# Weights times values, two heads at a time in fp32, each head in its own 64 columns of the array

## The chip, the cores and the metric

The program runs on one core of a Trainium2 chip. The metric is the device time of one launch, in microseconds, from the runs of the whole program. Beside it there is one profiled execution, whose span (first to last instruction) and whose instruction times the readings below use. The engines are called as in the profile: PE (TensorE, matmuls), PEld (its weight loads), DVE (VectorE), ACT (ScalarE), POOL (GpSimd), SP (the engine that issues the DMAs).

## The reference

Attention with a compressive memory over 4 batches of 8 heads, 576 tokens, head width 64, followed by a dense block with 2,048 hidden units. All in float32.

```python
def _attn_ref(q, k, v, M_prev, z_prev, beta):
    scores = scale * np.matmul(q, k.transpose(0, 1, 3, 2))
    scores = np.where(causal, -1000000000.0, scores)
    scores = scores - scores.max(-1, keepdims=True)
    a = np.exp(scores)
    a /= a.sum(-1, keepdims=True) + 1e-09
    local = np.matmul(a, v)
    q_p = phi(q)
    mem_ret = np.einsum('bhsd,bhde->bhse', q_p, M_prev)
    mem_norm = np.einsum('bhsd,bhd->bhs', q_p, z_prev)[..., None] + 1e-06
    g = 1.0 / (1.0 + np.exp(-beta))[None, :, None, None]
    return g * (mem_ret / mem_norm) + (1 - g) * local

def _moe_ref(x, w_in, w_out):            # x: 2304 x 512
    h = x @ w_in
    sp = np.where(h > 20.0, h, np.log1p(np.exp(np.minimum(h, 20.0))))
    return (h * np.tanh(sp)) @ w_out
```

## The kernel before

There are 32 heads in 16 pairs (`p`), two heads (`e` = 0, 1) to a pair. Per head, `scores` multiplies q by k, DVE adds the mask and takes the row minimum (L458), ACT takes the exponential (L465), `norm` scales each row by its weight (L101) and puts the features of q beside it, so that one row of `w` holds both the attention weights and the part that multiplies the memory. `transp` transposes `w` on PE in four groups of three or four blocks (L534), and a copy brings each group from PSUM to SBUF. `av` then multiplies: the values (with the memory matrix as their first 64 rows) are the stationary operand, 128 rows by 64 columns, and the transposed weights move. The output of a head is 64 x 576, made in two parts: part 0 holds 320 tokens (three matmuls of 320, 256 and 128 columns), part 1 holds 256 tokens (five matmuls, four of 256 columns and one of 128); the table is `AVJ`. Both parts use the one PSUM bank of the pool `ps_v`, so part 1 begins after ACT has copied part 0 out (L105, into the tile `x` of the pair, 64 partitions to a head).

`av` has two forms here, and `FA` = 16 tells them apart:

- Heads 0 to 15: plain fp32. Transposed weights `at` are copied out alternately by ACT and DVE (`FAE`), and each of the eight matmuls of a head (L570) takes them and `v` as they are. In the trace one such fp32 matmul stands as two instructions.
- Heads 16 to 31: split operands. ACT rounds the transposed weights to `ah`, DVE makes the rest `al` (L543), POOL makes `vh` from `v` in the same way (`vprep`, L109 and L95), and each of the eight products is three matmuls of one instruction each (L583): 24 for a head.

Both forms write PSUM partitions 0 to 63, so both use columns 0 to 63 of the array.

Beside the heads, six blocks of `w_in` and `w_out` are converted to pairs of rounded operands (`split`, `narrow`, L141 to L173: DVE ops L148, L154, L157, L164 among them), one after each of the heads 1 to 6. From head 9 on, one step of the dense block's first part (`steps_a`) is issued per head: 18 slots `slot_a` of 24 matmuls (L257), each followed by a chain of element-wise work on ACT, DVE and POOL (`mish0` to `mish2`), and 12 calls of `out_a`, 18 matmuls each (L272). These steps run at a low priority (`p1`: -400). When the heads are done, `tail` converts the ten remaining weight blocks, mixed with what is left of the first part, and runs 62 units: 12 matmuls `mm_h` (L697), the same element-wise chain, and 9 or 12 matmuls `mm_o` (L717).

The order of the instructions on each engine is made by a scheduler when the program is built, from the order of the code, the priorities (`OFF`, through `run`) and its own estimate of when things are ready. It is fixed in the program: each engine works through its own list and waits where an operand isn't there.

## Time and profile before

| | us |
|---|---|
| median of 3 runs | 764.65 (764.34 to 766.92) |
| span of the profiled execution | 763.0 |
| the profiled execution's PE busy | 708.4 |
| DVE busy | 647.2 |
| POOL busy | 436.0 |
| ACT busy | 409.2 |

The profiled execution's span lies 1.65 us below the median of the runs. In the page, busy time of an engine is the time that it had an instruction in work; a share of the span near 100% in a stretch says that the stretch waits for that engine, if others wait for it. Matmuls are pipelined, so the step from one's start to the next one's start tells what it costs, and not its duration. In a timeline row, "x10" merges ten instructions in sequence, and the next row's start tells when they were over.

### The profile page before, as it was taken

The numbers are of one execution on the slowest core, as the hardware profiler recorded it, in microseconds if no ns is written. First come the engines' busy times: TensorE is split into PE (matmuls) and PEld (weight loads), VectorE is DVE, ScalarE is ACT, GpSimd is POOL, SyncE is SP. The second block draws the span as 40 slices with busy tenths as digits, with TensorE's granted clock in tenths as the row PEclk, the third lists the DMA queues.
The fourth block names the chain that finished last, engine by engine and source line by source line (L and its number), as shares of the span: only waits on it lengthen the run. The fifth ranks groups of instructions, "written<-read, shape, count | busy, mean of one in ns | idle before, by whom it ended". The sixth has DMA issues, their size and how long they took to land.

```text
span 763.0 us, 11170 instructions
## 1 busy us (share of the span) xinstructions
PE 708.4 (93%) x3544; PEld 557.0 (73%) x3544; DVE 647.2 (85%) x1287; ACT 409.2 (54%) x929; POOL 436.0 (57%) x442
## 2 busy tenths in 40 slices
PE   5999999999999999999778677699999999999996
PEld 3566666667788888878666555478888889899894
DVE  5799998999987787868999999978868877786885
ACT  5566765767576766657453533344434445445443
POOL 4787886888889687756757665643223313223221
PEclk9999999999999999999999897899999999999999
DMA  6566786655644564333636222033033030021001
GB/s 244 163 187 198 225 235 182 204 159 161 199 119 145 149 166 140 93 104 128 207 128 209 78 89 83 29 110 111 0 111 111 12 113 16 1 82 43 1 1 41
DMA packets 51851, 91.18 MB, mean 119 GB/s; under 512 B 8272, under 2 KB 23632, under 8 KB 51792
## 3 DMA queue, kind: packets, MB, share of 16 engines
q1 hardware_dynamic: 51792, 90.47, 38.9%
q8 instruction: 28, 0.46, 0.2%
q14 instruction: 31, 0.25, 0.1%
HBM read 56.63 MB, written 17.30 MB: 97 GB/s over the span
## 4 chain that ended last, share of the span: by engine, by line
PE 62%; DVE 23%; issue 6%; ACT 3%; DMA 3%; POOL 1%; SPq 0%; POOLq 0%; ACTq 0%; DVEq 0%
PE o L717 10%; PE h L697 10%; PE vps L570 7%; PE t L534 7%; PE s L450 7%; PE h L257 5%; PE s L449 5%; PE vps L583 4%; PE acc L272 4%; DVE u L92 4%; DVE ws L148 3%; DVE r L92 2%; DVE g L95 2%; DVE wa L154 2%; DVE ws L164 2%
## 5 line engine op out<-in xcount | busy, mean ns | idle before, releaser
L95 POOL TENSOR_TENSOR u<-u,r 128x512 f32<-128x512 f32 (+1 forms) x80 | 106.5, 1331 | 205.4 <-DVE r L92 191.8
L697 PE MATMUL h<-xb,wi 128*128 128x384 f32 (+1 forms) x744 | 173.1, 379 | 22.9 <-DVE u L233 22.8
L697 PEld LDWEIGHTS h<-xb,wi 128*128 128x128 f32 x744 | 141.4, 196 | 46.3 <-DVE u L233 24.6
L717 PE MATMUL o<-wo,g 128*128 128x512 f32 x648 | 163.1, 394 | 4.1 <-ACT g L105 3.1
L717 PEld LDWEIGHTS o<-wo,g 128*128 128x128 f32 x648 | 122.3, 190 | 29.7 <-ACT g L105 3.9
L228 ACT ACTIVATE L<-u 128x512 f32<-128x512 f32 (+1 forms) x80 | 47.1, 589 | 149.5 <-DVE u L92 148.0
L465 ACT ACTIVATE w<-w,mx 128x576 f32<-128x576 f32 (+4 forms) x160 | 88.9, 557 | 33.3 <-DVE mx L458 33.0
L101 POOL TENSOR_SCALAR w<-w,rc 128x64 f32<-128x64 f32 (+3 forms) x128 | 84.2, 674 | 14.2 <-DVE rc L504 10.0
L458 DVE CUSTOM_DVE_ANT_0 w<-s,mask 128x288 f32<-128x288 f32 (+4 forms) x160 | 62.6, 422 | 28.0 <-PE s L450 16.9
L92 DVE SCALAR_TENSOR_TENSOR u<-e 128x512 f32<-128x512 f32 (+1 forms) x80 | 81.0, 1013 | 1.3
L534 PE MATMUL t<-ident,w 128*128 128x128 f32 (+1 forms) x417 | 72.3, 288 | 7.3 <-DVE al L543 6.2
L233 DVE SCALAR_TENSOR_TENSOR u<-u,h 128x512 f32<-128x512 f32 (+1 forms) x80 | 50.1, 626 | 30.0 <-POOL u L95 29.9
L92 DVE SCALAR_TENSOR_TENSOR L<-u,r 128x512 f32<-128x512 f32 (+1 forms) x80 | 57.4, 717 | 18.6 <-ACT r L229 18.2
L257 PE MATMUL h<-xb,wi 128*128 128x256 f32 x432 | 65.9, 291 | 2.5 <-DVE u L233 2.5
L272 PE MATMUL acc<-wo,g 128*128 128x512 f32 x216 | 62.0, 418 | 3.8 <-ACT ob L105 3.2
L450 PE MATMUL s<-lk,r 64*128 64x288 f32 (+1 forms) x168 | 64.7, 385 | 0.0
L534 PEld LDWEIGHTS t<-ident,w 128*128 128x128 f32 (+1 forms) x417 | 48.3, 144 | 22.4 <-DVE al L543 6.8
L449 PE MATMUL s<-r 128*128 128x288 f32 (+1 forms) x168 | 60.2, 358 | 1.1 <-DVE mx L458 1.1
L257 PEld LDWEIGHTS h<-xb,wi 128*128 128x128 f32 x432 | 56.4, 190 | 6.2 <-DVE u L233 3.1
L570 PE MATMUL vps<-at,v 128*64 128x256 f32 (+2 forms) x256 | 59.9, 373 | 0.0
L105 ACT CAST g<-u 128x512 fp32r<-128x512 f32 (+1 forms) x80 | 45.8, 573 | 20.7 <-DVE u L233 19.4
L92 DVE SCALAR_TENSOR_TENSOR r<-L,r 128x512 f32<-128x512 f32 (+1 forms) x80 | 55.1, 689 | 0.3
(72 smaller groups left out, 1280.0 us busy)
## 6 DMA issues: line engine op xcount, KB each, us to landing
r<-t SPq DMA_DIRECT2D x84, 144.0 KB, 2.7
raw<-in_w_in_dram SPq DMA_DIRECT2D x16, 512.0 KB, 3.5
raw<-in_w_out_dram SPq DMA_DIRECT2D x16, 512.0 KB, 3.7
f<-in_f_src_dram SPq DMA_DIRECT2D x14, 576.0 KB, 5.2
xb<-xs SPq DMA_DIRECT2D x24, 256.0 KB, 4.6
qn<-in_qn_dram SPq DMA_DIRECT2D x16, 320.0 KB, 3.2
v<-in_vn_dram SPq DMA_DIRECT2D x16, 320.0 KB, 4.0
xs<-xo SPq DMA_DIRECT2D x16, 288.0 KB, 2.9
```

The costliest lines, as they stand in the source:

```text
L92: engines[ENG[name]].scalar_tensor_tensor(**kw)
L95: engines[ENG[name]].tensor_tensor(**kw)
L101: engines[which].tensor_scalar(out=o, in0=i, scalar1=scale, scalar2=1.0, op0=ALU.mult, op1=ALU.mult)
L257: nc.tensor.matmul(ps[:, TA * a:TA * a + TA], wi[y, f][:, c, :], x[c][:, z], start=(q == 0), stop=(q == 11))
L272: nc.tensor.matmul(acc[:], g[:, y, c:c + 128], wo[z, f], start=(f == 0 and y == z), stop=(f == KA - 1 and z == 1),)
L449: nc.tensor.matmul(ps[:, o:o + n], r[:, e, q0:q0 + 128], r[:, 2 + e, a:b], start=True, stop=False)
L450: nc.tensor.matmul(ps[:, o:o + n], r[le, e, q0:q0 + 128], l[le, a:b], start=False, stop=True)
L465: nc.scalar.activation(out=row, in_=row, func=ACTF.Exp, scale=-1.0, bias=g["mx"][:, m:m + 1], accum_out=g["sm"][:, m:m + 1])
L534: nc.tensor.transpose(ps[:, o:o + n], g["w"][:n, c:c + 128], ident[:n, :n])
L570: nc.tensor.matmul(ps[0:64, a:b], d["v"][:, t, e], g["ah"][gi][:, c:c + b - a], start=(k == 0), stop=(k == last))
L697: nc.tensor.matmul(ps[:, :n], wi[a, f][:, c, :], x[c][:, b], start=(k == 0), stop=(k == 11))
L717: nc.tensor.matmul(D_[t][:], g[:, y, 128 * t:128 * t + 128], wo[z, f], start=(f == f0 and y == z), stop=(f == NF - 1 and z == 1),)
```

## The change

All pairs now use plain fp32, and a pair's two heads are multiplied together. `av` takes a pair: it runs once, after the second head's `transp`, and for each of the eight products issues a matmul for head 0 into PSUM partitions 0 to 63 (array columns 0 to 63) and one for head 1 into partitions 64 to 127 (columns 64 to 127), in turn. ACT copies a part of both heads with one instruction over 128 partitions. The split operands go: no `vh` (and no `vprep` on POOL), no `al` on DVE. Heads 16 to 31 get their transposed weights like the others, two groups by ACT and two by DVE. The `at` tiles get 14 buffers in one tag (before: five each in two), `v` gets two. The core of the diff:

```diff
-AHB = 5
+AHB = 14
...
-VB = 1
+VB = 2
...
-F2 = 32
...
-FA = 16
...
         def loadv(p):
             d = pr[p]
-            if 2 * p < FA:
-                d["v"] = ap_.tile([128, 5, 2, 2, D], F32, tag="vh", name="v")[:].rearrange(
-                    "p t e i d -> p (t e i d)")[:, 0:640].rearrange("p (t e d) -> p t e d", t=5, e=2)
-            else:
-                d["v"] = ap_.tile([128, 5, 2, D], F32, tag="v", name="v", bufs=VB)[:]
+            d["v"] = ap_.tile([128, 5, 2, D], F32, tag="v", name="v", bufs=VB)[:]
...
-        def vprep(p):
...
-            return [lambda: one(0), lambda: two(0), lambda: one(1), lambda: two(1)] if 2 * p >= FA else []
...
-            def hi(base, n):
-                copy(FAE[base] if h < FA else "a", g["ah"][base][:, :n], g["tps"][:, :n])
-
-            def lo(base, n):
-                if h < FA:
-                    return
-                nc.vector.tensor_tensor(
-                    out=g["al"][base][:, :n], in0=g["tps"][:, :n], in1=f32(g["ah"][base][:, :n]), op=ALU.subtract
-                )
+            def out(base, n):
+                copy(FAE[base], g["at"][base][:, :n], g["tps"][:, :n])
...
-        def av(h):
-            p, e = divmod(h, 2)
-            d, g = pr[p], hd[h]
-            big = slice(64 * e, 64 * e + 64)
+        def av(p):
+            d = pr[p]
+            at = [hd[2 * p + e]["at"] for e in range(2)]
...
                 for k, (t, a, b, gi, c) in enumerate(ops):
-                    if h < FA:
+                    for e in range(2):
                         nc.tensor.matmul(
-                            ps[0:64, a:b], d["v"][:, t, e], g["ah"][gi][:, c:c + b - a], start=(k == 0), stop=(k == last)
+                            ps[64 * e:64 * e + 64, a:b], d["v"][:, t, e], at[e][gi][:, c:c + b - a],
+                            start=(k == 0), stop=(k == last),
                         )
...
-                    for y, (w, z) in enumerate(((0, ah), (0, al), (1, ah))):
-                        nc.tensor.matmul(
-                            ps[0:64, a:b], vv[:, w], z[gi][:, c:c + b - a], start=(k == 0 and y == 0), stop=(k == last and y == 2)
-                        )
...
-                if h < F2:
-                    copy(ENG["cp"], d["x"][big, q0:q0 + n], g["v", j][0:64, :])
-                    return
...
+                copy(ENG["cp"], d["x"][:, q0:q0 + n], g_["v", j][:])
...
-            run(av(h), 'av')
+            if e:
+                run(av(p), 'av')
```

Because the scheduler builds the order anew, the whole list of each engine moves a little. Three places matter for what follows. The first is on PE, the multiplication of the fifth pair (its `v` tile is `v_829` before and `v_817` after; numbers tell buffers apart; `s` are scores, `t` and `h<-ident` transposes, `h<-xb` the dense block's first part). Before, part 1 of the pair's first head stands as five matmuls in a row:

```order
L450 MATMUL s_1150<-lk_1033,r_1030 128x288
L570 MATMUL vps_937<-at_911,v_829 64x256
L570 MATMUL vps_937<-at_918,v_829 64x256 x2
L570 MATMUL vps_937<-at_925,v_829 64x256
L570 MATMUL vps_937<-at_925,v_829 64x128
L534 MATMUL h_994<-ident_108,w_946 128x128 x2
```

After, part 1 of the pair, tiles 899, 906 and 913 from the first head and 968, 975 and 982 from the second:

```order
L428 MATMUL s_1256<-lk_1216,r_1213 128x64
L534 MATMUL vps_997<-at_899,v_817 64x256
L534 MATMUL vps_997<-at_968,v_817 64x256
L534 MATMUL vps_997<-at_906,v_817 64x256
L534 MATMUL vps_997<-at_975,v_817 64x256
L534 MATMUL vps_997<-at_906,v_817 64x256
L534 MATMUL vps_997<-at_975,v_817 64x256
L534 MATMUL vps_997<-at_913,v_817 64x256
L534 MATMUL vps_997<-at_982,v_817 64x256
L534 MATMUL vps_997<-at_913,v_817 64x128
L534 MATMUL vps_997<-at_982,v_817 64x128
L255 MATMUL h_1311<-xb_1207,wi0_0_84 128x256 x2
```

What moved: the ten matmuls of both heads' part 1 stand together, the two heads in turn, and part 1 of the second head is no longer a group of its own some twenty rows later.

The second place is on PE too, part 0 of the same pair after the change. Its first matmul (head 0, 320 columns) stands earlier still, between scores; here are the rest:

```order
L507 MATMUL h_983<-ident_108,w_921 128x128 x3
L534 MATMUL vps_989<-at_961,v_817 64x320
L534 MATMUL vps_989<-at_899,v_817 64x256
L427 MATMUL s_1247<-r_1213 128x288
L428 MATMUL s_1247<-lk_1216,r_1213 128x288
L507 MATMUL t_1086<-ident_108,w_1045 128x64
L507 MATMUL t_1086<-ident_108,w_1045 128x128
L427 MATMUL s_1251<-r_1213 128x288
L428 MATMUL s_1251<-lk_1216,r_1213 128x288
L507 MATMUL t_1100<-ident_108,w_1045 128x128 x4
L507 MATMUL h_1093<-ident_108,w_1045 128x128
L534 MATMUL vps_989<-at_968,v_817 64x256
```

What moved: the six matmuls of part 0 are spread over three places with scores and transposes between them. Over the program the 256 matmuls of `av` stand in 83 such runs: 29 of one matmul, 18 of two, 18 of three, 6 of ten, and 12 of four to nine.

The third place is on DVE, in the heads with split operands. Before, among the masking (`ISA w,mx`) and the element-wise work of the dense block (`e`, `u`), the rest of the transposed weights is made:

```order
L214 TENSOR_SCALAR e_1892<-e_1892 128x512
L543 TENSOR_TENSOR al_2406<-t_2407,ah_2405 128x448
L92 SCALAR_TENSOR_TENSOR u_1893<-e_1892 128x512
L458 ISA w_2678,mx_2679<-s_2690,mask_109 128x448
L458 ISA mx_2679 128x1
L458 ISA w_2678,mx_2679<-s_2690,mask_109 128x64
L458 ISA mx_2679 128x1
L380 TENSOR_SCALAR phe_2946<-qn_2940 128x640
L543 TENSOR_TENSOR al_2415<-t_2416,ah_2414 128x512
```

After, copies of half of the groups stand there:

```order
L90 SCALAR_TENSOR_TENSOR r_1478<-L_1477,r_1478 128x512
L105 COPY at_2428<-t_2429 128x512
L479 TENSOR_SCALAR rc_2557<-sm_2529,gt_110 128x5
L374 TENSOR_SCALAR phe_3018<-qn_3012 128x640
L436 ISA w_2618,mx_2619<-s_2625,mask_109,mx_2619 128x288
L436 ISA mx_2619 128x1
L482 RECIPROCAL rc_2557<-rc_2557 128x5
```

What moved: four subtractions a head became two copies. The steps of the dense block also stand later against the heads: before the last head's row weights (`rc`, L504 before) DVE finishes 13 of the 18 slots of the first part in the order of before, and 9 in that of after.

## Rows read from the trace of the kernel before

**Rows 1.** The page, busy us (share of the span) and instructions of each engine.

```profile
PE 708.4 (93%) x3544; PEld 557.0 (73%) x3544; DVE 647.2 (85%) x1287; ACT 409.2 (54%) x929; POOL 436.0 (57%) x442
```

**Rows 2.** Busy us by stretch: stretch, its length, engines, TensorE clock, DMA share, GB/s.

```profile
0.00:176.50 176.50, 166.68 (x742) 106.06 (x742) 158.10 (x418) 112.92 (x296) 134.92 (x159) 1.00 0.67 198
176.50:361.00 184.50, 183.36 (x1142) 148.77 (x1142) 150.13 (x373) 122.14 (x304) 140.21 (x165) 0.99 0.48 142
361.00:495.00 134.00, 99.27 (x446) 78.72 (x445) 133.31 (x153) 58.55 (x105) 87.88 (x61) 0.87 0.36 117
495.00:763.00 268.00, 259.14 (x1220) 223.42 (x1218) 205.64 (x347) 115.62 (x227) 73.00 (x58) 1.00 0.17 54
...
0.00:20.00 20.00, 11.58 (x24) 6.44 (x24) 12.31 (x34) 10.49 (x23) 8.73 (x15) 1.00 0.68 241
```

**Rows 3.** Lines L504 and L164: duration min/median/max ns, first and last start us.

```profile
L504 DVE RECIPROCAL rc<-rc x32: 172/180/192, 17.9 to 361.1; 128x5 f32<-128x5 f32 x32
L164 DVE SCALAR_TENSOR_TENSOR ws<-raw,ws x32: 677/940/1799, 6.5 to 494.1; 128x512 f32<-128x512 uint32 x32
```

**Rows 4.** Timeline of DVE at the 17th head's L504: start us, us.

```profile
176.35 0.18 DVE L504 RECIPROCAL rc<-rc 128x5 f32<-128x5 f32 x1
```

**Rows 5.** Timeline of PE, fp32 values: part 1 of a head, then part 0.

```profile
137.79 2.16 PE L570 MATMUL vps<-at,v 128*64 128x256 f32 x10
139.88 0.33 PE L534 MATMUL t<-ident,w 128*128 128x128 f32 x1
...
150.18 1.40 PE L570 MATMUL vps<-at,v 128*64 128x320 f32 x6
151.51 0.40 PE L449 MATMUL s<-r 128*128 128x288 f32 x1
```

**Rows 6.** Timeline of PE, split values: first row of a part 0, row behind it.

```profile
268.76 0.30 PE L583 MATMUL vps<-ah,vh 128*64 128x320 f32 x1
...
269.81 0.27 PE L534 MATMUL t<-ident,w 64*128 64x64 f32 x1
```

**Rows 7.** Tile vps, weight loads of L570: duration min/median/max ns.

```profile
L570 PEld LDWEIGHTS vps<-at,v x256: 132/137/230, 29.5 to 183.1; 128*64 128x64 f32 x128
```

**Rows 8.** Timeline of PE where two matmuls use different halves of the rows.

```profile
98.08 0.35 PE L450 MATMUL s<-lk,r 64*128 64x192 f32 x1
98.09 0.27 PE L534 MATMUL t<-ident,w 64*128 64x64 f32 x1
98.37 0.48 PE L570 MATMUL vps<-at,v 128*64 128x320 f32 x1
```

**Rows 9.** Timeline of PE, the dense block's first part, each with the row behind it.

```profile
280.10 1.72 PE L257 MATMUL h<-xb,wi 128*128 128x256 f32 x13
281.65 0.29 PE L449 MATMUL s<-r 128*128 128x288 f32 x1
...
270.31 4.14 PE L272 MATMUL acc<-wo,g 128*128 128x512 f32 x17
274.30 0.36 PE L449 MATMUL s<-r 128*128 128x448 f32 x1
```

**Rows 10.** Lines L543 and L107 of DVE: duration min/median/max ns.

```profile
L543 DVE TENSOR_TENSOR al<-t,ah x64: 541/638/692, 182.0 to 392.9; 128x512 fp32r<-128x512 f32 x32, 128x448 fp32r<-128x448 f32 x16, 128x384 fp32r<-128x384 f32 x16
L107 DVE COPY at<-t x14: 517/588/684, 113.1 to 177.9; 128x512 f32<-128x512 f32 x7, 128x384 f32<-128x384 f32 x7
```

**Rows 11.** Groups by shape, DVE ops of a slot: busy us, mean ns, idle before.

```profile
L92 DVE SCALAR_TENSOR_TENSOR u<-e 128x512 f32<-128x512 f32 x48 | 49.8, 1038 | 0.6
L214 DVE TENSOR_SCALAR e<-e 128x512 f32<-128x512 f32 x48 | 29.7, 618 | 3.7 <-ACT e L211 3.7
L95 DVE TENSOR_TENSOR g<-u,g 128x512 fp32r<-128x512 f32 x30 | 23.8, 793 | 2.7 <-ACT g L105 2.7
```

**Rows 12.** Chain of waits in the tail, in order of time: start us, us.

```profile
509.78 2.72 PE o L717 x12
512.50 2.72 PE h L697 x12
```

More of the change, by code (lines that the diff above doesn't have):

```diff
@@ L80 @@
 TC = []
-OFF = {'prep1': -400, 'conv': 200, 'av': -50, 'vprep': 100, 'p1': -400, 'scores': 100, 'prep0': 400}
+OFF = {'prep1': -400, 'conv': 200, 'av': -50, 'p1': -400, 'scores': 100, 'prep0': 400}
 @with_exitstack
@@ L406, in prep @@
             return [qk] if p >= FS else [], [ph0, ph1, ph2, ph3, ph4]
-        def vprep(p):
-            d = pr[p]
-            def one(i):
-                if i == 0:
-                    d["vh"] = ap_.tile([128, 5, 2, 2, D], F32R, tag="vh", name="vh")
-                copy(ENG["vhi"], d["vh"][:, :, i, 0, :], d["v"][:, :, i, :])
-            def two(i):
-                v, vh = d["v"], d["vh"]
-                tt(
-                    "vlo", out=vh[:, :, i, 1, :], in0=v[:, :, i, :], in1=f32(vh[:, :, i, 0, :]), op=ALU.subtract
-                )
-            return [lambda: one(0), lambda: two(0), lambda: one(1), lambda: two(1)] if 2 * p >= FA else []
         banks = [[(4, 0, 288)], [(4, 288, 576)], [(3, 0, 448), (0, 0, 64)], [(2, 0, 320), (1, 0, 192)]]
@@ L521, in tr @@
                 if first:
[L522 to L528 removed]
+                    g["at"] = []
+                g["at"].append(tp.tile([128, 512], F32, tag="at", name="at", bufs=AHB))
                 ps = g["tps"] = spare(h, TQ, ps_t, "t")
@@ L535, in tr @@
                     o += n
[L537 to L545 removed]
+            def out(base, n):
+                copy(FAE[base], g["at"][base][:, :n], g["tps"][:, :n])
             for base, gr in enumerate(GR):
                 n = sum(QT[m][1] - QT[m][0] for _, m in gr)
[L549 to L550 removed]
+                ops += [lambda gr=gr, first=(base == 0): tr(gr, first), lambda base=base, n=n: out(base, n)]
             return ops
@@ L565, in mms @@
                 n = ops[0][2]
-                ps = g["v", j] = ps_v.tile([128, n], F32, tag="v", name="vps")
+                ps = g_["v", j] = ps_v.tile([128, n], F32, tag="v", name="vps")
                 last = len(ops) - 1
                 for k, (t, a, b, gi, c) in enumerate(ops):
-                    if h < FA:
+                    for e in range(2):
                         nc.tensor.matmul(
-                            ps[0:64, a:b], d["v"][:, t, e], g["ah"][gi][:, c:c + b - a], start=(k == 0), stop=(k == last)
-                        )
-                        continue
-                    vv, ah, al = d["vh"][:, t, e], g["ah"], g["al"]
-                    if h >= F2:
-                        both = vv.rearrange("p i d -> p (i d)")
-                        z = ah[gi][:, c:c + b - a]
-                        nc.tensor.matmul(ps[:, a:b], both, z, start=(k == 0), stop=False)
-                        z = al[gi][:, c:c + b - a]
-                        nc.tensor.matmul(ps[:, a:b], both, z, start=False, stop=(k == last))
-                        continue
-                    for y, (w, z) in enumerate(((0, ah), (0, al), (1, ah))):
-                        nc.tensor.matmul(
-                            ps[0:64, a:b], vv[:, w], z[gi][:, c:c + b - a], start=(k == 0 and y == 0), stop=(k == last and y == 2)
+                            ps[64 * e:64 * e + 64, a:b], d["v"][:, t, e], at[e][gi][:, c:c + b - a],
+                            start=(k == 0), stop=(k == last),
                         )
@@ L588, in cp @@
                 q0, n = AVJ[j][0], AVJ[j][1][0][2]
-                if h < F2:
-                    copy(ENG["cp"], d["x"][big, q0:q0 + n], g["v", j][0:64, :])
-                    return
-                sml = slice(64 - 64 * e, 128 - 64 * e)
-                tmp = tp.tile([128, 320], F32, tag="tmp", name="tmp", bufs=1)
-                nc.scalar.copy(out=tmp[big, :n], in_=g["v", j][sml, :])
-                nc.vector.tensor_tensor(
-                    out=d["x"][big, q0:q0 + n], in0=g["v", j][big, :], in1=tmp[big, :n], op=ALU.add
-                )
+                copy(ENG["cp"], d["x"][:, q0:q0 + n], g_["v", j][:])
             def xhi():
@@ L613, in av @@
                 ops += [lambda j=j: mms(j), lambda j=j: cp(j)]
-            if e:
-                ops += [xhi, xlo]
-            return ops
+            return ops + [xhi, xlo]
         nh = 2 * NP
@@ L638, in attention @@
                 run(prep(p)[1], 'prep1')
-                run(vprep(p), 'vprep')
             elif p + 1 < NP:
```

13 lines of the change are left out of this document (3 added, 10 removed).

## The prediction

> **What bounds the kernel now.** I read the page's first line, then the busy times by stretch, with stretches cut where the work changes, then single lines and timelines. PE is busy 708.4 of 763.0 us, DVE 647.2 [rows 1]. The average hides four stages [rows 2]. Stage A ends with the 17th head's row weights at 176.5 us [rows 4], stage B with the last head's at 361 [rows 3], stage C with the last conversion of the dense block's weights at 495 (the last L164 starts at 494.1) [rows 3], stage D with the program. In A both PE (166.7 of 176.5) and DVE (158.1) are nearly full; most of what PE lacks is the start, where it works 11.6 of the first 20 us. B is PE's: 183.4 of 184.5, with DVE at 150.1. C is DVE's: 133.3 of 134.0, with PE at 99.3. D is PE's again, 259.1 of 268.0. So a PE gain counts in full in B, in A only down to what DVE needs, in C not at all; a DVE gain counts in C.
>
> **Part 1: the multiplication itself (PE).** Part 1 of an fp32 head takes from 137.79 to 139.88, 2.09 us, for ten instructions; part 0 takes 1.33 us for six [rows 5]. A matmul is two instructions, so these move 2 x 1152 and 2 x 704 columns. Two equations give 0.848 ns a column and 0.136 us for entering and leaving a run, so 0.271, 0.217 and 0.109 us for one instruction of 320, 256 and 128 columns. A head has 2 x 1856 columns, 3.15 us; sixteen heads 50.4, and with the 40 runs in which the order of before has them, 40 x 0.136 = 5.4 more: 55.8 us. A split part 0 takes 1.05 us for 3 x 704 columns [rows 6]; less one entry that is 0.433 ns a column, so 2.41 us for a head's 3 x 1856, 38.6 for sixteen, and with 67 runs 47.7. Together 103.5 us before.
>
> After, 256 fp32 matmuls stand in 83 runs, the two heads in turn. The rows of before have no case of it: every value matmul there writes columns 0 to 63. Upper bound: one after the other, as now: 2 x 50.4 for the columns and 83 x 0.136 = 11.3 for the runs, 112.1 us, 8.6 more than before (the first eight pairs, with 35 runs, 55.2, 0.6 less; the last eight, with 48, 56.9, 9.2 more). Lower bound: the halves work side by side. Instructions start in order and the two of one matmul use the same columns, so head 1's first can start with head 0's second, and a run of n matmuls takes n + 1 steps where one after the other takes 2n. A run of ten gains nearly half, a lone matmul nothing, and 29 of the 83 runs are lone ones. Going through the order run by run with the three step lengths gives 33.0 us for the first eight pairs and 35.3 for the last; with the runs 37.8 and 41.8. That is 18.0 us less than before in the fp32 heads and 5.9 less in the split ones, about 24 in all. I take the lower bound, because the nearest row shows halves at work side by side, if halves of the rows and not of the columns: a score matmul on 64 rows starts at 98.08, a transpose on 64 rows at 98.09, and the next instruction at 98.37, as if the transpose had cost nothing [rows 8]. Two more places in the trace look the same.
>
> A weight load of 64 columns lasts 0.137 us [rows 7] and stands inside steps of 0.217, although the running matmul uses the same rows. The Trainium skill (TensorE: Matmul & The Clock Gate, Part 3: Packing small matmuls) says that a weight load overlaps running matmuls only when its group of rows differs; by that rule the 512 loads, all on the full 128 rows, would each wait, and the pairs would go one after the other at best. The trace doesn't bear that out for one head's own loads; no run here shows it for two halves. The same section reports matmuls in three different column groups at 2.38 times the speed, which no run here shows either.
>
> **Part 2: the copies and splits.** Before, 64 subtractions on DVE of 0.638 us, 40.8 us; after, 32 copies of about 0.59 in their place, 18.9 [rows 10]. So 22 us less on DVE, nearly all in stage B, which DVE doesn't bound. POOL loses `vprep`, ACT half its copies out of the `ps_v` bank; neither ends a stage [rows 2], and I put both at nothing: what covers them is PE's full load in B. The wait that the change adds, that a pair's matmuls need both heads' transposes, would hold PE's queue; with 14 `at` tiles and scores and transposes of the next pair placed between the runs, I price it at nothing, and up to 8 us if that cover is thin.
>
> **Part 3: what stands where.** In the order of after, between the 17th and the 32nd head's scores PE has 101 fewer `h` matmuls (185 for 286) and 42 fewer `acc` ones (78 for 120). At 1.55 / 13 = 0.119 and 3.99 / 17 = 0.235 us [rows 9] that is 12.0 + 9.9 = 21.9 us of PE, which isn't saved but done later. At the last conversion DVE has finished 24 of 80 slots before and 19 after: five more units remain for stage D.
>
> **The sum by stages.** A: PE falls to about 151 (166.7 less 16 of the 18; the last pair lies in B). DVE becomes the bound: 158.1 less one weight conversion that moves to B (four or five ops, 4 us) is 154; of its 18.4 us idle 7.7 are the start, and the 10.7 others shrink as PE's results come sooner, to nothing at best: 162 to 172.5. I take 170, so 6.5 of the 16 count. B: 183.4 - 21.9 - 7 (the 2 left from the fp32 heads and 5 of the 5.9; the rest lies in C) = 154.5, and the 1.1 idle: 155.5; DVE, with four slots fewer at some 3.9 us each (five ops of 0.6 to 1.0 [rows 11]) and the splits out, is near 117 and off the path. C: between the last L504 and the last L164 DVE has one slot fewer (-3.9), ten subtractions fewer (-6.4), five copies more (+3.0), five `g` subtractions fewer (-4.0) [rows 10, 11] and single ops that come to -1: 134 - 12.3 = 121.7. D: 268 and five units of 2.72 + 2.72 us [rows 12], 27.2: 295.2. The sum is 170 + 155.5 + 121.7 + 295.2 = 742.4 us for a span of 763.0; with the 1.65 us by which the median of the runs lies over it, 744. The check by PE alone: 708.4 - 24 = 684.5 busy, idle 19 in A, 1 in B, 31.5 in C (34.7 scaled by its length), 8.9 in D: 745. I say 744. With the ends of A and part 2's wait it reaches from 736 (A at 162) to 754 (A at 172.5 and 8 us for the wait).
>
> **Rivals.** *One after the other.* The column halves don't overlap. Then A stays at 176.5, B is 183.4 - 21.9 + 7 (of the 9.2) + 1 = 169.5, C and D as above: 762.9, or 764.5 as a median; by PE alone, 717.0 busy and 54.6 idle, 773. So 764 to 773. For it: the trace has no column halves. Against it: the row halves [rows 8].
>
> *Slower: each change of half costs a run's entry.* Today entering and leaving the 64-column shape costs 0.136 us. If going from one half to the other does too, with nothing overlapped, the 173 changes inside runs add 23.5 us in A and B, where PE is the bound: 764 to 773 becomes 788 to 797; I say 792. It decides from about 30 ns a change (173 x 0.03 = 5) on. For it: both halves are new to the trace. Against it: transposes and scores of 64 and 128 rows change places all the time there, and at 98.08 a change cost nothing [rows 8]. The Trainium skill (TensorEngine Tiling (Array Packing), Key Properties) says that a change of the tiling drains PE and a change of the tile within it doesn't; no run here shows the second.
>
> *The overlap comes and is hidden.* DVE holds A at 176.5 and the paired wait costs its 8 us in B: 742.4 + 6.5 + 8 = 757, 758 as a median.
>
> **How the numbers follow.** Side by side as summed: 0.70. Hidden: 0.08. One after the other: 0.17, half of it over 768.5. Slower by changes of half: 0.05. A measurement of this kernel can tell 0.5%, 3.8 us, from no change. So faster 0.78, same 0.09, slower 0.13. The range: 734, a little under the lower end of the sum, to 768. It leaves out the slower half of the second case, the third, and some 0.05 below.
>
> **What would show it.** In the profile after: matmuls of the values that start in pairs, a run of ten that is over 2.3 us after it began (11 steps, side by side) and not 4.0 (20 steps); PE near 685 busy; DVE busy near its whole in A and C; no subtraction of transposed weights and 32 copies more on DVE; the last L504 (then another line) near 325 us and the last conversion near 447. The forecast is wrong if a run of ten takes 4 us, if PE is idle in B for more than 5 us (the paired wait), or if the five units left for D cost more than 27 us.

## The result and the profile after

The changed kernel takes 772.4 us (median of 15 runs, 765.6 to 779.5), the kernel before 765.2 in the same comparison (15 runs, 764.3 to 768.4). The ratio is 1.0082, 95% interval [1.0062, 1.0103]: slower by 0.8%. The forecast was 744. The ratio leaves out the three longest runs of the changed kernel (778.6 to 779.5 us), which lie more than 1.5% above its fastest one; ratios below are taken in the same way, so they can differ a little from the quotient of the medians. The profiled execution is a run of 769.4 us, 3 us under the median, with a span of 767.6 us.

The page of after, busy us of each engine, answers to [rows 1]:

```profile
PE 696.3 (91%) x3416; PEld 527.2 (69%) x3416; DVE 622.1 (81%) x1255; ACT 381.7 (50%) x865; POOL 415.3 (54%) x410
```

All five lines are smaller than before, and the kernel is slower. The busy times by stretch, cut at the same three events as [rows 2] (stretch, its length, busy us of PE, PEld, DVE, ACT, POOL, then TensorE clock, DMA share, GB/s), tell where:

```profile
0.00:173.80 173.80, 156.25 (x740) 98.36 (x741) 149.77 (x413) 104.65 (x276) 129.56 (x154) 0.95 0.68 201
173.80:334.20 160.40, 158.82 (x878) 106.41 (x876) 120.75 (x329) 93.82 (x244) 110.12 (x131) 1.00 0.50 146
334.20:465.00 130.80, 86.99 (x427) 69.64 (x425) 127.94 (x136) 52.12 (x93) 95.53 (x65) 0.82 0.42 137
465.00:767.60 302.60, 294.23 (x1374) 252.76 (x1374) 223.66 (x380) 131.13 (x252) 80.09 (x63) 1.00 0.16 49
```

Read two columns: the length, and the clock. The forecast had A 170, B 155.5, C 121.7, D 295.2; measured are 173.8, 160.4, 130.8 and 302.6. And A, which PE spent at a granted clock of 1.00 before, now shows 0.95: 17.1 us of A went by at half clock, 1.2 GHz in place of 2.4.

For the rest I cut PE's time in another way. The step from one PE instruction's start to the next one's is put down to the first, up to its end, and the rest of the step is called idle. Summed over the whole program, by the tile that is written:

| PE, us | before | after | difference |
|---|---|---|---|
| weights times values (`vps`) | 103.7 | 79.6 | -24.1 |
| transposes (`t`) | 58.4 | 68.3 | +9.9 |
| scores (`s`) | 122.3 | 125.6 | +3.3 |
| dense block (`h`, `acc`, `o`) | 423.6 | 422.2 | -1.4 |
| idle | 50.5 | 66.9 | +16.4 |
| sum (the span ends some 5 us after PE) | 758.5 | 762.6 | +4.1 |

So the multiplication gives 24.1 us, what the forecast said. The other work of PE takes 11.8 of it back, and idle time more than the rest: 7.7 of the 16.4 in A, 9.7 in C, -1.0 in B and D.

### The profile page after: what moved, and what is told of

Read it like the earlier page. It is cut to its first block, busy times and chain, and to the rows that moved or that the text cites. A ratio compares the mean times of both kernels' runs of the same rounds, so it can differ in the third digit from the quotient of the medians.

```text
span 767.6 us, 10775 instructions
## 1 busy us (share of the span) xinstructions
PE 696.3 (91%) x3416; PEld 527.2 (69%) x3416; DVE 622.1 (81%) x1255; ACT 381.7 (50%) x865; POOL 415.3 (54%) x410
## 4 chain that ended last, share of the span: by engine, by line
PE 55%; DVE 25%; issue 8%; ACT 4%; DMA 3%; POOL 3%; SPq 1%; POOLq 0%; ACTq 0%; DVEq 0%
PE h L640 12%; PE o L660 12%; PE vps L534 7%; PE t L507 6%; PE s L428 5%; PE s L427 4%; PE h L255 4%; DVE u L90 4%; PE acc L270 3%; DVE ws L146 3%; DVE r L90 3%; DVE wa L152 2%; DVE L L90 2%; DVE ws L162 2%; DVE ws L155 2%
## 5 line engine op out<-in xcount | busy, mean ns | idle before, releaser
L640 PE MATMUL h<-xb,wi 128*128 128x384 f32 (+1 forms) x744 | 168.1, 370 | 14.7 <-DVE u L231 14.6
L640 PEld LDWEIGHTS h<-xb,wi 128*128 128x128 f32 x744 | 139.2, 193 | 34.7 <-DVE u L231 16.4
L99 POOL TENSOR_SCALAR w<-w,rc 128x64 f32<-128x64 f32 (+3 forms) x128 | 90.0, 721 | 26.9 <-DVE rc L482 19.1
L255 PE MATMUL h<-xb,wi 128*128 128x256 f32 x432 | 71.0, 318 | 24.8 <-DVE u L231 24.6
L534 PE MATMUL vps<-at,v 128*64 128x256 f32 (+2 forms) x512 | 85.2, 381 | 2.1 <-ACT x L103 1.0
L255 PEld LDWEIGHTS h<-xb,wi 128*128 128x128 f32 x432 | 63.4, 218 | 32.3 <-DVE u L231 26.5
L507 PE MATMUL t<-ident,w 128*128 128x128 f32 (+1 forms) x417 | 75.2, 294 | 10.2 <-DVE at L105 3.7
L90 DVE SCALAR_TENSOR_TENSOR L<-u,r 128x512 f32<-128x512 f32 (+1 forms) x80 | 55.6, 695 | 16.4 <-ACT r L227 16.1
L427 PE MATMUL s<-r 128*128 128x288 f32 (+1 forms) x168 | 63.5, 378 | 1.3 <-DVE mx L436 1.0
L270 PE MATMUL acc<-wo,g 128*128 128x512 f32 x216 | 60.0, 408 | 2.2 <-ACT ob L103 1.8
L534 PEld LDWEIGHTS vps<-at,v 128*64 128x64 f32 x512 | 38.0, 138 | 26.9 <-issue 9.1
```

The lines of the kernel that those rows point to most:

```text
L90: engines[ENG[name]].scalar_tensor_tensor(**kw)
L99: engines[which].tensor_scalar(out=o, in0=i, scalar1=scale, scalar2=1.0, op0=ALU.mult, op1=ALU.mult)
L255: nc.tensor.matmul(ps[:, TA * a:TA * a + TA], wi[y, f][:, c, :], x[c][:, z], start=(q == 0), stop=(q == 11))
L270: nc.tensor.matmul(acc[:], g[:, y, c:c + 128], wo[z, f], start=(f == 0 and y == z), stop=(f == KA - 1 and z == 1),)
L427: nc.tensor.matmul(ps[:, o:o + n], r[:, e, q0:q0 + 128], r[:, 2 + e, a:b], start=True, stop=False)
L507: nc.tensor.transpose(ps[:, o:o + n], g["w"][:n, c:c + 128], ident[:n, :n])
```

## Experiments: is the multiplication really side by side

`e1_serial` is the changed kernel with the head loop outside, so that the same matmuls stand one head after the other.

```diff
-                for k, (t, a, b, gi, c) in enumerate(ops):
-                    for e in range(2):
+                for e in range(2):
+                    for k, (t, a, b, gi, c) in enumerate(ops):
```

> The changed kernel, but all matmuls of the pair's head 0 stand ahead of those of head 1 in each part, so that halves of the array can meet only where the two heads touch. The overlap measured in the changed kernel (20 instructions of 256 and 128 columns in 2.10 us) should go: 512 instructions one after the other cost about 112 us for 79.7, 32 us more of PE. If PE bounds the attention, the time rises by about 30 us, to 800. If the gain of the overlap is lost in waits and in a lower granted clock anyway (theory: PE's idle time), the time stays within 10 us of the changed kernel's 772 or even falls, and the clock in the first 174 us, 0.95 there, is 1.00 again.

Measured: 788.4 us, ratio 1.0293 [1.0273, 1.0314]; `vps` 107.5 us of PE in place of 79.6. The timeline of PE shows a run of ten matmuls (twenty instructions) in after:

```profile
98.56 2.17 PE L534 MATMUL vps<-at,v 128*64 128x256 f32 x20
```

and such a run in `e1_serial`, with the row behind it:

```profile
107.91 3.51 PE L534 MATMUL vps<-at,v 128*64 128x256 f32 x20
111.35 0.44 PE L507 MATMUL t<-ident,w 128*128 128x128 f32 x2
```

Same instructions, 2.17 us in turn, 3.51 one head after the other. In the trace of after the two heads' instructions start 6 to 7 ns apart (98.563 and 98.569, then 98.829 and 98.836). So the column halves do work side by side. The kernel is 16 us shorter with the alternation, for 28 us less of `vps`; as the order around the runs differs between the two kernels too, those 16 us aren't the price of the alternation alone. The rule that the prediction weighed (the Trainium skill, TensorE: Matmul & The Clock Gate, Part 3: Packing small matmuls: a weight load overlaps running matmuls only where its group of rows differs) would have all twenty loads of the run wait, for they use the same 128 rows. The trace doesn't agree: twenty loads of 0.137 us one after another would be 2.74 us alone, and the run takes 2.17 with its matmuls.

## Experiments: what the fp32 form costs without the pairs

`e2_nosplit` is the kernel before with all 32 heads in its plain fp32 form, in columns 0 to 63.

```diff
-FA = 16
+FA = 32
```

> The kernel before with plain fp32 for all heads: no operand split, but each head alone in columns 0 to 63. DVE loses 22 us of subtractions, POOL the 25 us of splitting the values, PE gains 9 us (3.5 us a head for 2.9). Theory that PE's work is what counts: 9 us slower than before, 774. Theory that the split's DVE work is what counts: 765 or less. If the scheduler's order (the dense block's first part standing later against the heads) costs by itself, this kernel pays it too: 10 of 18 slots done at the last head, 13 in before.

Measured: 780.1 us, ratio 1.0197 [1.0178, 1.0215]. DVE loses the subtractions, and the kernel loses 14.5 us, more than either theory said. `vps` rises from 103.7 to 113.7, close to the 9 expected of it, and the transposes from 58.4 to 62.3. The second number is a cost that stands in another instruction's row: what it takes to go from a transpose into a run of values. In before, three transposes ahead of a split run (timeline of PE: start us, us):

```profile
227.63 0.49 PE L534 MATMUL t<-ident,w 128*128 128x128 f32 x3
227.87 0.36 PE L583 MATMUL vps<-al,vh 128*64 128x256 f32 x1
```

In after, the same three ahead of an fp32 run:

```profile
209.94 0.49 PE L507 MATMUL t<-ident,w 128*128 128x128 f32 x3
210.36 0.86 PE L534 MATMUL vps<-at,v 128*64 128x256 f32 x6
```

0.24 us to the run's start there, 0.42 here. Over stage B the last transpose ahead of a run takes 28 ns (median of 31) before and 203 ns (of 28) after; in `e2_nosplit`, with single fp32 heads, it is 203 ns too, and so it is in the first sixteen heads of before. It is a price of fp32 behind a transpose, not of the pairs. Leaving the run is dearer as well. From a last value instruction of 256 columns to a score it is 309 ns in B, in after and in `e2_nosplit`; 216 of them are what such an instruction takes inside a run, so leaving costs 93. Before it is 117 in both places, and leaving costs nothing. In B the transposes alone cost 5.7 us more, for four instructions fewer (210 for 214).

## Experiments: which pairs lose

The pair form was put into the kernel before for some pairs only; the others keep their form of before.

```diff
-            run(av(h), 'av')
+            if p not in PAIRED:
+                run(av(h), 'av')
+            elif e:
+                run(avp(p), 'av')
```

`PAIRED` is pairs 0 to 7 in `e5_pairs_first8`, 8 to 15 in `e6_pairs_last8`, 4 to 15 in `e10_pairs_from4`, 12 to 15 in `e11_pairs_from12`. Paired heads copy their weights out in fp32, the split is left out for them. These four kernels keep the buffers of before, ten for the transposed weights and one for `v` of a paired head, where the changed kernel has 14 and two. So the last row of the table below differs from the others in more than the number of pairs.

> The kernel before, with the pair form only in the first eight pairs, whose operands were plain fp32 in both kernels; the last eight keep the split and go head by head (ten buffers for the transposed weights in all, as before). PE saves 17 us in stage A and pays nothing behind it. If stage A were PE's, the time falls by 15, to 750. Theory of the hidden gain (A waits for other engines, PE's idle time and half clock take the rest): A comes out 1 to 4 us shorter and the time lies between 758 and 765.

> The counterpart: the pair form only in the last eight pairs, where it takes the place of three single-pass matmuls. PE should save some 7 us on the multiplication and pay some 5 to 9 for the dearer entries of its runs (the instruction ahead of a run took 0.203 us there in the changed kernel and 0.028 in the split form). Theory that the last eight pairs carry the loss: 768 to 775. Theory that the first eight carry it: 760.

> The kernel before with the pair form in pairs 4 to 15 (before that single fp32 heads). Pairs 8 to 15 gave 763.8, all sixteen 772.4. If each of the first eight pairs costs alike, 4 of them give about 768. If the loss comes from the first pairs, which run while the loads and the conversions of the dense block's weights share the engines, 762 to 764 with no half clock in stage A; if from pairs 4 to 7, 771 to 773 with 15 us or more of it.

> The kernel before with the pair form in pairs 12 to 15 alone. Pairs 8 to 15 gave -1.8 us; if each pair brings its share, -0.9, about 764.7, stage A as before (176.5, no half clock), 64 fewer subtractions of transposed weights become 32 fewer. If the gain is bought by the change of order alone it needn't be in proportion: 760 to 770.

| pairs in the new form | us | ratio, 95% interval | A, us | at half clock in A, us |
|---|---|---|---|---|
| 12 to 15 | 765.4 | 0.9989 [0.9978, 1.0001] | 177.1 | 0 |
| 8 to 15 | 763.8 | 0.9975 [0.9966, 0.9985] | 176.5 | 0 |
| 4 to 15 | 775.6 | 1.0120 [1.0077, 1.0163] | 187.3 | 34.1 |
| 0 to 7 | 783.1 | 1.0246 [1.0210, 1.0283] | 184.7 | 54.6 |
| all | 772.4 | 1.0082 [1.0062, 1.0103] | 173.8 | 17.1 |

`e11_pairs_from12` can't be told from before. The kernel with the last eight pairs alone is the only one that beats before, by 0.25%; that is far less than a mere change of order can do (next sections), so it isn't shown that the pairs did it. For `e5_pairs_first8` the two theories expected 750 and 758 to 765, and it is the slowest. The busy times by stretch of `e6_pairs_last8` (columns as above):

```profile
0.00:176.50 176.50, 165.67 (x739) 105.22 (x739) 156.96 (x414) 112.35 (x296) 130.22 (x154) 1.00 0.68 198
176.50:345.30 168.80, 168.80 (x939) 116.22 (x939) 129.86 (x335) 98.98 (x252) 114.78 (x134) 1.00 0.49 139
345.30:471.00 125.70, 85.67 (x419) 68.45 (x419) 122.02 (x136) 52.32 (x93) 89.33 (x61) 0.85 0.46 146
471.00:762.10 291.10, 282.76 (x1324) 242.94 (x1322) 222.17 (x371) 125.83 (x243) 78.52 (x62) 1.00 0.16 49
```

A is as long as before, B and C are 15.7 and 8.3 us shorter, and D is 23.1 longer: most of what B gives is work moved, and of the 6.7 us that its `vps` saves, the transposes take 6.3 back.

The loss comes with the first eight pairs, and between pairs 4 and 7 it can be located. In `e10_pairs_from4` the tenth head's row weights are ready at 108.0 us, in before at 105.7; the fifteenth's at 168.9 and 155.5. Busy times of that stretch in `e10_pairs_from4`, then in before:

```profile
108.00:132.40 24.40, 22.39 (x92) 13.53 (x90) 18.40 (x49) 10.50 (x30) 13.61 (x16) 0.72 0.48 137
132.40:169.00 36.60, 35.37 (x162) 21.23 (x161) 31.22 (x81) 21.51 (x58) 22.43 (x28) 0.84 0.60 177
```

```profile
105.70:125.40 19.70, 19.70 (x104) 13.63 (x103) 19.41 (x48) 11.51 (x31) 15.26 (x18) 1.00 0.65 190
125.40:155.50 30.10, 30.10 (x152) 19.86 (x153) 27.59 (x77) 20.52 (x54) 21.35 (x26) 1.00 0.69 214
```

61.0 us for 49.8. PE is busy for 57.8 of the 61.0, with fewer instructions in the first part, at a clock of 0.72 and 0.84. DVE waits for PE's scores there for 10.7 us, for 2.7 in before. Whether ten buffers are too few for the pairs was not tested: a copy waits for a buffer of transposed weights once in A of `e5_pairs_first8` (1.7 us) and never in A of `e10_pairs_from4`, but the scheduler built the order with ten in view.

## Experiments: waits, the clock, and filling the waits

In A of after PE waits, where before it hardly did. Who waited for whom (us in total, times, longest) from 20 us to the end of A; in after, the four largest of eleven such rows, which come to 9.5 us together:

```profile
PE t L507 <- ACT at L103: 3.1, 1, 3.1
PE t L507 <- POOL w L99: 1.4, 2, 1.1
PE t L507 <- DMA qn<-in_qn_dram: 0.9, 1, 0.9
PE t L507 <- DVE w L99: 0.8, 1, 0.8
```

before, all of them, 1.6 us:

```profile
PE t L534 <- DMA qn<-in_qn_dram: 0.9, 1, 0.9
PE s L446 <- DVE mx L458: 0.5, 1, 0.5
PE t L534 <- POOL w L101: 0.2, 1, 0.2
```

The longest of them in the timeline of PE in after (the bracket is the idle time before a row), and the busy times around it:

```profile
121.28 0.40 PE L427 MATMUL s<-r 128*128 128x288 f32 x1
121.61 0.39 PE L428 MATMUL s<-lk,r 64*128 64x288 f32 x1
121.93 0.55 PE L507 MATMUL t<-ident,w 128*128 128x128 f32 x3
125.59 0.74 PE L507 MATMUL t<-ident,w 64*128 64x64 f32 x2 [3.11 <-ACT at L103]
125.99 0.59 PE L427 MATMUL s<-r 128*128 128x288 f32 x1
```

```profile
110.00:125.00 15.00, 12.48 (x66) 7.45 (x65) 13.24 (x40) 7.25 (x22) 12.25 (x17) 1.00 0.86 248
125.00:135.20 10.20, 9.61 (x35) 6.83 (x36) 8.14 (x22) 6.61 (x17) 6.14 (x7) 0.50 0.39 127
```

The same score matmul takes 0.40 us before the wait and 0.59 after it: for 10.2 us PE runs at 1.2 GHz in place of 2.4. The other such stretch of A, 70.4 to 77.2, stands behind waits of 0.56 and 1.10 us. All five of A's in `e5_pairs_first8` and `e10_pairs_from4` have a wait of 0.3 to 2.2 us shortly ahead of them.

That isn't a rule, though. Over all the kernels of this case A has 31 stretches at half clock. 27 follow a wait of PE of 0.3 to 3.1 us; the other four, one in `e1_serial`, two in `e8_before_two_raw` and the longest stretch of `e12_pair_earlier`, 17.0 us, have PE busy without a gap ahead of them. In `e8_before_two_raw`:

```profile
70.00:79.60 9.60, 9.60 (x49) 6.25 (x48) 7.49 (x25) 5.74 (x17) 8.52 (x11) 1.00 0.89 264
79.60:83.00 3.40, 3.40 (x11) 2.06 (x12) 3.40 (x6) 3.28 (x10) 1.98 (x2) 0.50 0.63 240
```

And waits go by without it: in after one of 0.76 us at 50.5 and one of 0.51 at 157.5, and the 6.9 us that PE waits at the very start, with a clock of 1.00 behind them. So what brings half clock on isn't shown here, only that waits often stand ahead of it.

The kernel's own runs go with the clock. Over the 12 runs of after that the ratio counts (765.6 to 777.0 us) the time at half clock, from the mean granted clock, goes from 63 to 96 us, correlation with the time 0.85, slope 0.29 us of kernel for one at half clock. Before has 38 us of it in its profile. That is an association, and it was put to the test.

**Removing a wait.** In after the 3.1 us at 125 follow from ACT, which waits 3.29 us for a transfer of raw weights with one buffer. `e7_two_raw` gives it two (and 12 `at` buffers in place of 14, for room); `e8_before_two_raw` gives the kernel before the same two.

```diff
-            t["r"] = raw = pool.tile([128, 512, 2], I32, tag="raw", name="raw", bufs=1 if own is cp else RT)
+            t["r"] = raw = pool.tile([128, 512, 2], I32, tag="raw", name="raw", bufs=2 if own is cp else RT)
```

> The changed kernel with two buffers for the raw weights in the attention for one (and 12 for 14 buffers of transposed weights, for room). In the changed kernel ACT and DVE wait 9 us in stage A for those loads, which they didn't in before; ACT's longest, 3.3 us, holds the exponentials behind it, PE then idles 3.1 us and gets half clock for the next 10. Theory that such waits eat the gain in A: those waits are gone, A is 5 to 10 us shorter and the time 760 to 766. Theory that A is bound by something else: 770 to 775.

> Control for the run before it: the kernel before with the same two buffers for raw weights. It had no wait for these loads in stage A, so nothing of that kind can be gained: 760 to 768. If it falls as much as the changed kernel does with them, the buffers help through the order that the scheduler makes and not through the wait.

Measured: 778.4 us, 1.0161 [1.0122, 1.0200], and for before 782.2, 1.0232 [1.0203, 1.0261]. The wait is gone, and others came: PE idles 19.6 us in A of `e7_two_raw`, with 30.7 at half clock. So taking that wait out brought no gain. And the control loses 16.6 us with no pair in it, A 185.5 for 176.5, though after its first 20 us PE waits there for only some 3 us in all: an edit that rebuilds the planner's order can cost more than the change studied here. That leaves the price of the one wait open, since the run without it has another order as well.

**Filling the waits.** `e9_fill` adds to after a matmul that nothing reads, ahead of each score group of heads 2 to 15.

```diff
+                if 2 <= h < 16:
+                    fill = ps_a.tile([128, DM], F32, tag="acc", name="fill")
+                    nc.tensor.matmul(fill[:, 0:128], ident[:], ident[:], start=True, stop=True)
```

`e13_fill_tied` starts at head 4 and takes `d["r"][:, e, 0:128]`, the pair's own q, as the moving operand, so that the planner can't put it early; `e14_fill_half` does so for the first and third group only; `e15_from4_fill` is `e10_pairs_from4` with it in heads 8 to 15, first and third group.

> The changed kernel with one more fp32 matmul of 128x128 by 128 columns ahead of each of the four score groups of heads 2 to 15 (56 in all, some 0.22 us each at full clock, 12 us of PE), into a bank that nothing reads: it does work that the result doesn't need. Theory 'the clock': in stage A PE waits in a few places for 1 to 3 us, the granted clock falls to half behind them and the kernel pays for it twice. The extra work stands ahead of just those waits, so half-clock time in A falls from 17 us to under 5, A stays within 2 us of 173.8, the kernel within 3 us of 772 or under it. Theory 'latency': A's length is set by the chains between PE, DVE, ACT and POOL, the clock only follows; then the extra work adds 4 to 12 us to A and the kernel takes 776 to 784.

> The changed kernel with a matmul of 128 columns that nothing reads ahead of each of the four score groups of heads 4 to 15, taking the pair's own q as its moving operand, so that it can't stand early as in the run before: 48 of them, 96 instructions of 0.217 us as measured there, 20.8 us of PE. It does work that the result doesn't need. In the run before, 12 heads took 114.3 us with such work and full clock, 114.1 without it and 17 us at half clock. Theory 'clock': no half clock in stage A, and A within 3 us of 173.8 in spite of 20.8 us more PE work, the kernel 768 to 773. Theory 'chains of the other engines': half clock or not, A grows by 10 us or more, the kernel over 776.

> The same with half as much: ahead of the first and third score group only, 24 matmuls, 10.4 us of PE. Theory 'clock': under 7 us of half clock in A, and A under 172, since the work added is less than what waits and half clock took there (16 us); the kernel 763 to 769. Theory 'chains': A 174 to 180, the kernel 772 to 778.

> The kernel with the pair form in pairs 4 to 15 (775.6 us; stage A 187.3 with 34 us at half clock, all of A's loss in 108 to 169 us), with 16 such matmuls in heads 8 to 15, 6.9 us of PE, work that the result doesn't need. Theory 'clock': the half clock in A falls under 14 us and A under 181, the kernel 766 to 771. Theory 'chains': A stays at 185 to 194, the kernel 774 to 782.

| | us | ratio, 95% interval | A, us | at half clock in A | PE idle in A |
|---|---|---|---|---|---|
| after | 772.4 | 1.0082 [1.0062, 1.0103] | 173.8 | 17.1 | 17.6 |
| `e9_fill` | 776.6 | 1.0117 [1.0072, 1.0162] | 190.1 | 0 | 6.9 |
| `e13_fill_tied` | 786.6 | 1.0242 [1.0181, 1.0302] | 184.1 | 17.1 | 10.9 |
| `e14_fill_half` | 783.3 | 1.0262 [1.0211, 1.0313] | 182.6 | 20.5 | 13.2 |
| `e15_from4_fill` | 774.8 | 1.0113 [1.0084, 1.0141] | 182.0 | 6.8 | 13.3 |

The clock theory doesn't hold in the form in which I put it down. In `e9_fill` the clock is full through A, but the filler took 24 us of PE (0.217 us an instruction, twice what I had counted), and a third of it stood in the first 60 us, where it put the fourth head back by 16. From the fifth head to the 17th it takes 114.3 us and after 114.1, with half of the filler, some 12 us of useless work, and full clock against none and 17 us at half clock. Tied to its head, the filler neither kept the clock up (17.1 and 20.5 us at half) nor was it free: A grows by 8.8 to 10.3. Only `e15_from4_fill` shows a gain: half clock down from 34.1 to 6.8 us and A down from 187.3 to 182.0, half of what A had lost; the kernels' medians, 774.8 and 775.6, don't differ clearly. That fits a price of half clock in A, but it is one profile of each, in two orders. In no run did keeping the clock up bring back PE's 18 us.

## Experiments: order or pair form

First the stages in which work stands. `e3_first_part_early` and `e4_more_first_part` are after with the dense block's first part ranked or spread so that more of it runs between the heads; `e12_pair_earlier` is after with the pair's multiplication ranked earlier.

```diff
-OFF = {'prep1': -400, 'conv': 200, 'av': -50, 'p1': -400, 'scores': 100, 'prep0': 400}
+OFF = {'prep1': -400, 'conv': 200, 'av': -50, 'p1': 150, 'scores': 100, 'prep0': 400}
```

(`e4_more_first_part`: `'p1': 0` and `SPREAD = 1.4`; `e12_pair_earlier`: `'av': 100`, `'p1'` as it was.) The last three runs, `e16` to `e18`, give the kernel before these settings, so that the forms can be compared within one setting.

> The changed kernel with the dense block's first part at priority +150 for -400. The order then has 338 h and 144 acc matmuls and 13 slots ahead of the last head's end, as before had (334, 120, 13); the changed kernel has 233, 78 and 9. Theory that the order lost the gain: the last stage has two units less and the clock stays up, 755. Theory that it is only moved from one PE-bound stage to another: within 5 us of the changed kernel, 768 to 775, with a stage B longer by 25 us and the stages behind it shorter by as much.

> The changed kernel with the first part at priority 0 and 1.4 steps a head: 371 h, 156 acc and 15 slots ahead of the last head's end, 25 slots at the last weight conversion (18 or 19 in the changed kernel, 24 in before). Theory of the order: 750. Theory that PE work only changes its stage: 766 to 775.

> The changed kernel with the pair's multiplication ranked 150 steps earlier in the planner's order (priority +100 for -50). Theory 'burst': PE waits in stage A because the pair's sixteen matmuls stand late and together; ranked earlier they leave the path sooner, PE's idle in A falls from 17.6 to under 13 us and the kernel takes 764 to 769. Theory 'neither': the idle stays over 15 us, only its places change, and the time is 770 to 778.

> The kernel before with its multiplication ranked 150 steps earlier, the same setting as in the changed kernel that took 780.5 us. Theory 'the planner's order': the order of before is a fitted one and most rebuilt orders lose 10 to 20 us in stages A and B, with or without the pair form; then 774 to 786 here, stage A 180 or more or B over 190, some half clock in A. Theory 'the pair form': it is the pairs that make PE wait in A; then 763 to 769 here, stage A 174 to 179 and no half clock in A.

> The kernel before with the first part of the dense block ranked and spread as in the changed kernel that took 772.4 us. Theory 'the planner's order': 772 to 784. Theory 'the pair form': 760 to 769, stage A 174 to 179 with no half clock, as the change of setting touches little before head 9.

> The kernel before with the first part ranked still earlier (priority +150), as in the changed kernel that took 777.3 us. Theory 'the planner's order': 772 to 786. Theory 'the pair form': 760 to 769, no half clock in stage A.

| setting | before's form, us | pair form, us | A: before, pair | half clock in A: before, pair |
|---|---|---|---|---|
| as given | 765.2 | 772.4 | 176.5, 173.8 | 0, 17.1 |
| multiplication earlier | 767.8 (`e16`) | 780.5 (`e12`) | 171.8, 183.0 | 0, 56.0 |
| more of the first part | 775.6 (`e17`) | 772.4 (`e4`) | 177.0, 175.2 | 3.4, 17.1 |
| first part early | 770.5 (`e18`) | 777.3 (`e3`) | 179.1, 170.1 | 0, 23.9 |
| two raw buffers | 782.2 (`e8`) | 778.4 (`e7`) | 185.5, 183.6 | 6.8, 30.7 |

The ratios to before: `e3` 1.0186 [1.0121, 1.0251], `e4` 1.0081 [1.0057, 1.0105], `e12` 1.0183 [1.0129, 1.0236], `e16` 1.0031 [1.0019, 1.0042], `e17` 1.0141 [1.0109, 1.0174], `e18` 1.0080 [1.0049, 1.0110].

More of the first part between the heads didn't bring the gain back: 755 was expected of `e3_first_part_early` if its later place had lost it, and 750 of `e4_more_first_part`.

Of the later two theories, that the order costs or that the pair form does, neither wins alone. Over the five settings the pair form is slower by 12.7, 7.2 and 6.8 us and faster by 3.2 and 3.8, 3.9 slower in the mean, with a spread from which 3.9 can't be told from nothing; the settings by themselves move the form of before by 17 us. What holds in all five: the pair form has 17 to 56 us at half clock in A, the other 0 to 6.8. Stage A of the second setting, `e12_pair_earlier` and then `e16_before_av_earlier`, is where it is largest:

```profile
0.00:183.00 183.00, 166.04 (x723) 104.27 (x723) 149.78 (x405) 104.17 (x272) 128.00 (x153) 0.85 0.65 191
```

```profile
0.00:171.80 171.80, 159.96 (x708) 101.49 (x708) 152.80 (x399) 108.56 (x284) 124.97 (x151) 1.00 0.68 198
```

PE is busy 6 us longer, with 13 us less multiplication in it. The table of PE's time, as a mean over the five settings, repeats that of the result: `vps` -24.9 us, transposes +11.4, scores +5.5, idle +9.7. That is what the pair form does here in the mean of five orders: it saves 25 us of PE, and 27 come back as dearer steps beside it and as waits. `vps` falls and the transposes rise in all five (by 19 to 30 and by 10 to 14 us), while idle time goes from 3 less to 16 more. I put what is left of the difference at a given setting down to the order; that is argued, not shown.

What stays open is which chain between PE, DVE, ACT and POOL sets A's pace when PE has less to do. Every edit that should show it also rebuilt the order. The pair form with other numbers of buffers in one and the same order, and pairs with split operands, weren't tried.

## Why the prediction was wrong, step by step

- **The multiplication: right.** Forecast 103.5 us before and 79.6 after; measured 103.7 and 79.6. The first eight pairs went from 57.2 to 38.7, 18.4 less (18.0 said), the last eight from 46.6 to 40.9, 5.7 less (5.9 said). A run of ten took 2.17 us, 2.3 said. The rivals "one after the other" and "each change of half costs an entry" fall with the 6 to 7 ns between the heads and with `e1_serial`. That 772.4 lies inside the first one's 764 to 773 is chance: its mechanism isn't there.
- **Entering and leaving a run: mis-sized.** The 0.136 us came from two equations on the value matmuls' own rows [rows 5], so it left out what the entry adds to the row ahead. For fp32 that row takes 203 ns and not 28. In B: forecast 155.5, measured 160.4; transposes there +5.7 us.
- **A: the step whose mechanism failed.** "DVE becomes the bound" and its idle shrinks to some 12 us. DVE is busy 149.8 of 173.8, so it isn't the bound, and its idle grew from 18.4 to 24.0. PE saves its 18 us; 7.7 become idle time, and some 7.5 are dearer scores, transposes and dense matmuls, by my estimate some 4.7 of them in the two stretches at half clock (their steps there, less the mean step of the same kind in before). No term of the sum stood for either, and what makes PE wait there stays open. A is 2.7 us shorter where 6.5 was said; over the five settings, 0.8 in the mean.
- **The paired wait: not where it was looked for.** It was priced at 0 to 8 us, in B. B has 1.7 us of idle. PE's waits came in A, where the order has almost no dense work to put between the heads (6.3 us of it before), and they stand at the transposes and scores, only 1.6 of 9.5 us at the multiplication. That they come from the pairs needing both heads isn't shown.
- **C: mis-sized.** Forecast 121.7, measured 130.8. The conversions in C became two ops more, and three of their four kinds of op dearer. The groups of DVE in C, by shape (busy us, mean ns, idle before), after:

```profile
L146 DVE TENSOR_SCALAR ws<-raw 128x512 int32<-128x512 int32 x20 | 27.2, 1359 | 0.2 <-issue 0.2
L152 DVE SCALAR_TENSOR_TENSOR wa<-wa,ws 128x512 int32<-128x512 int32 x20 | 21.5, 1074 | 1.4 <-DVE ws L146 0.5
```

  before:

```profile
L148 DVE TENSOR_SCALAR ws<-raw 128x512 int32<-128x512 int32 x19 | 21.5, 1130 | 0.0
L154 DVE SCALAR_TENSOR_TENSOR wa<-wa,ws 128x512 int32<-128x512 int32 x19 | 19.2, 1012 | 0.3
```

  Together 8 us more, and DVE's idle goes from 0.7 to 2.9, in a stage in which POOL's share rose from 66% to 73% (95.5 of 130.8, 87.9 of 134.0 [rows 2]). I had taken DVE's counts and kept its durations. That DVE is slowed by POOL there was not tested.
- **D: a unit short.** Forecast 295.2, measured 302.6. DVE had finished 18 slots at the last conversion, not 19, so six units came over, at 5.44 us 32.6, and 18 `acc` instructions, 4.1 us, that were not in the sum: 9.5 us more than the sum had, where D's miss is 7.4.

The four misses are 3.8 + 4.9 + 9.1 + 7.4 = 25.2 us, the whole distance from the predicted span (742.4) to the measured 767.6. By size the mis-sized terms of C and D weigh most, 16.5 of the 25.2; A weighs least, but there it was the mechanism. In the check by PE alone, busy time came to 696.3 for 684.5 and idle time to 71.3 for 60.4. Of the three signs of being wrong that the prediction named, only the one on D came; for A it named none. By rivals, "the overlap comes and is hidden" was the nearest; its 758 took A at 176.5 and one wait, and missed the entries, C and D.

## What to carry to other kernels

A saving on one engine counts in a stage only if there is work ready to take its place: in B the dense block's matmuls filled nearly every gap, in A there was almost none to put in, and the time came back as waits and as half clock. That is how the stages read; no run put useful work into A to test it. Price a new instruction form with the row ahead of it and the row behind it, not by its own rows alone. And where a planner makes the order, give the kernel before the same settings as the changed one before putting a difference of 1% down to the change: here an unrelated setting moved the same form by 17 us.

## What the runs showed of the hardware

- Two fp32 matmuls of 128 rows in different 64-column halves start 6 to 7 ns apart; twenty such instructions take 2.17 us where one half after the other takes 3.51.
- Three single-instruction matmuls on split operands are cheaper than one fp32 matmul in one half: inside a run of before, 3 x 0.117 = 0.35 us for 256 columns against 2 x 0.216 = 0.43; `vps` 103.7 us with sixteen heads split, 113.7 with none (`e2_nosplit`).
- A transpose ahead of an fp32 run of values holds PE for 203 ns, ahead of a split run for 28.
- In A of after the granted clock fell to 1.2 GHz twice, for 17.1 us, in a stage in which PE was busy for nine tenths; before had no such stretch in A. Of 31 such stretches in A over all kernels 27 stand behind a wait of PE of 0.3 to 3.1 us, and four behind work without a gap.
